# Reading one word per row group of four weight matrices at the start of a fused recurrence and FFN kernel

## The chip, the core and the metric

The kernel runs on one core of one Trainium2 chip. Five engines work side by side, each through its own list of instructions in order: TensorE (PE in the profile; PEld is its weight load), VectorE (DVE), ScalarE (ACT), GpSimd (POOL) and SyncE (SP), which here only issues DMAs. ScalarE also issues a few DMAs. All of them run on the same 16 DMA engines. The metric is the device time of one execution in microseconds, the median of several runs.

## The reference

Two stages follow one another. The first is a gated recurrence over 768 time steps for 4 batches and 8 heads of width 48; the second is a max-out feed-forward layer over the 3072 resulting tokens of width 384, with 768 hidden units.

```python
for t in range(S):
    state = alpha[:, :, t, :, None] * state + np.einsum('bhd,bhe->bhde', k[:, :, t], v[:, :, t])
    y[:, :, t] = np.einsum('bhd,bhde->bhe', q[:, :, t], state)
...
x = np.ascontiguousarray(attn_out.transpose(0, 2, 1, 3)).reshape(B * S, H * D)
h = np.maximum(np.maximum(x @ w1, x @ w2), x @ w3)
return (h @ w_out).astype(np.float32)
```

q, k, v and alpha are 4 x 8 x 768 x 48; w1, w2 and w3 are 384 x 768; w_out is 768 x 384. All are float32 in memory.

## The kernel before

The tokens are cut into 12 steps of 256 tokens. Step s is block s // 4 of time of batch s % 4, so the recurrence of a batch goes on four steps later. Inside a step the recurrence is worked in chunks: running sums of the logarithms of alpha (by a matmul with a triangle of ones), keys and queries scaled by the exponentials of these sums, scores and outputs by matmuls, and a state of 16-bit floats per batch that is updated by matmuls. The transposed output xT then goes through the three gate matmuls (`gate`, L396), a maximum on ScalarE and VectorE (`maxed`, L409 and L411) and the projection (`project`, L420), and is scaled and stored (`store`).

Each piece of work has a letter, and the order is written out by hand in three strings: `PROLOGUE` (L470, steps 0 to 2 with the early pieces of the following ones), `STEADY` and `LAST`. `@` gives the step. TensorE, VectorE, ScalarE, GpSimd and SyncE each run their own pieces in the order of these strings. `H` pieces are filler matmuls on a blank tile (`warm`, L440), a fixed number of them.

The pieces that stand at the start:

- `load` (L93) reads 256 tokens of one of alpha, q, k, v: 384 KB in pieces of 384 bytes, on SyncE's queue, into a ring of four buffers per tensor (ra, rq, rk, rv in the profile).
- `load_const` (L114) reads two constants on ScalarE's queue: `cp` (128 rows of 1032 bytes: triangle, identity and mask as 16-bit floats) and `c32` (128 rows of 16 bytes; c in the profile).
- the string at L118 sets the first order: alpha of step 0, the constants, then k, q and v of step 0. After that `PROLOGUE` issues alpha and k of step 1, alpha of step 2, q and v of step 1, alpha of step 3, k and q of step 2, alpha of step 4, and then the first four weight pieces (`K0 K2 K1 K6`).
- `load_weight` (L102) reads a weight piece of 384 KB on SyncE's queue into its own staging tile (ws); `cast_weight` (L160) turns it into 16-bit floats on ScalarE or GpSimd. The weights are read in twelve pieces; the first three of `w1`, `w2`, `w3` take columns 0 to 255 of every row.
- `pair_decay` (L184, tile pa) multiplies neighbouring alphas, `inverse` (L193, L195) and `logs` (L188, tile la) take logarithms and exponentials on ScalarE, `near_q` (L203) and `scaled` (L235, tile qk) form the scaled queries and keys, `values` (L156, tile vt) the scaled values, `sums` (L209) the sums on TensorE.

The tile layer gives each DMA one of eight semaphores in turn, over both queues together, in the order in which the DMAs are written. A DMA whose semaphore was used before waits, on its issuing engine, until the DMA eight places earlier has landed.

Of the kernel before, what the change touches and what calls it, by code (L numbers as in the profile page):

```python
# [9 lines left out]
FP32 = mybir.dt.float32  # L10
# [13 lines left out]
def kernel(  # L24
# [12 lines left out]
    nc = tc.nc  # L37
# [4 lines left out]
    P = 128  # L42
# [38 lines left out]
    cpool = ctx.enter_context(tc.tile_pool(name="const", bufs=1))  # L81
# [28 lines left out]

    cp = cpool.tile([P, 2 * P + 2 * U + R * P], FP16, name="cp")
    c32 = cpool.tile([P, 4], FP32, name="c32")

    def load_const(*_):  # L114
        nc.scalar.dma_start(cp, nc.inline_tensor(cp_np, name="cp").ap())
        nc.scalar.dma_start(c32, nc.inline_tensor(c32_np, name="c32").ap())

    for item in """  # L118
        a0 c k0 q0 v0
    """.split():  # L120
        if item[0] == "c":
            load_const()
        elif item[0] == "w":
            load_weight(int(item[1:]))
        else:
            load(item[0], int(item[1:]))
# [420 lines left out]
```

## Time and profile before

| | us |
|---|---|
| median of 11 runs | 156.33 |
| lowest and highest run | 154.99, 160.23 |
| profiled execution, its own time | 156.39 |
| its span, first to last instruction | 154.6 |
| TensorE busy | 145.7 |
| VectorE busy | 121.6 |
| GpSimd busy | 84.6 |
| ScalarE busy | 77.8 |

The DMA queues carry this (packets, MB, share of the time of 16 DMA engines; q1 is SyncE's queue, q10 ScalarE's, q8 the fetch of instructions):

```profile
q1 hardware_dynamic: 72576, 31.89, 82.9%
q8 instruction: 21, 0.34, 0.9%
q10 hardware_dynamic: 432, 0.23, 0.8%
```

In the profile a line of a timeline gives the start, the length, the engine, the line of the code, the operation and the tiles (out<-in); in brackets stands how long the engine was idle before, and what ended that. "SPq" and "ACTq" are the instruction queues of SyncE and ScalarE, where DMAs are issued: the length is that of the issue, not of the transfer. The 40 slices of the page are 3.9 us each.

### The profile page before, as it was taken

The numbers are of one execution on the slowest core, as the hardware profiler recorded it, in microseconds if no ns is written. First come the engines' busy times: TensorE is split into PE (matmuls) and PEld (weight loads), VectorE is DVE, ScalarE is ACT, GpSimd is POOL, SyncE is SP. The second block draws the span as 40 slices with busy tenths as digits, with TensorE's granted clock in tenths as the row PEclk, the third lists the DMA queues.
The fourth block names the chain that finished last, engine by engine and source line by source line (L and its number), as shares of the span: only waits on it lengthen the run. The fifth ranks groups of instructions, "written<-read, shape, count | busy, mean of one in ns | idle before, by whom it ended". The sixth has DMA issues, their size and how long they took to land.

```text
span 154.6 us, 6225 instructions
## 1 busy us (share of the span) xinstructions
PE 145.7 (94%) x2691; PEld 108.6 (70%) x2691; DVE 121.6 (79%) x212; ACT 77.8 (50%) x156; POOL 84.6 (55%) x123
## 2 busy tenths in 40 slices
PE   6999875999999999999999999999999999999990
PEld 2446453878877698687787786886877877868850
DVE  2256985899989789889799799697896995885560
ACT  3578945762773386383582573553835614132221
POOL 5328799736919307928848659379388573010000
PEclk9999999999999999999999999999999999999999
DMA  5999999999989899999999999999909609411023
GB/s 120 321 325 326 274 306 302 328 338 313 332 219 279 221 274 262 234 146 314 211 238 273 166 244 317 134 298 274 213 6 73 169 4 105 137 55 51 6 100 104
DMA packets 73035, 32.52 MB, mean 210 GB/s; under 512 B 65456, under 2 KB 73008, under 8 KB 73008
## 3 DMA queue, kind: packets, MB, share of 16 engines
q1 hardware_dynamic: 72576, 31.89, 82.9%
q8 instruction: 21, 0.34, 0.9%
q10 hardware_dynamic: 432, 0.23, 0.8%
q14 instruction: 6, 0.05, 0.1%
HBM read 23.73 MB, written 4.72 MB: 184 GB/s over the span
## 4 chain that ended last, share of the span: by engine, by line
PE 83%; DVE 4%; DMA 3%; SPq 2%; issue 2%; POOL 1%; ACT 1%; ACTq 0%; DVEq 0%; POOLq 0%
PE gps L396 47%; PE ops L420 15%; PE yps L330 6%; PE yps L311 4%; PE aps L280 4%; DMA ra<-in_alpha_dram 3%; PE sps L369 3%; PE tps L259 2%; SPq L95 2%; DVE lat L287 2%; PE wps L440 2%; POOL qk L235 1%; PE lps L209 1%; DVE pa L184 1%; ACT ob L156 1%
## 5 line engine op out<-in xcount | busy, mean ns | idle before, releaser
L396 PE MATMUL gps<-xT,wcat 128*128 128x256 f16 x648 | 78.0, 273 | 0.0
L396 PEld LDWEIGHTS <-wcat 128*128 128x128 f16 x648 | 60.8, 98 | 10.1 <-issue 0.3
L411 DVE TENSOR_TENSOR hT<-gps,h 128x512 f16<-128x512 f32 x36 | 24.4, 687 | 11.5 <-PE gps L396 11.4
L287 DVE TENSOR_TENSOR lat<-aps,cp 128x512 f16<-128x512 f32 x48 | 30.6, 679 | 2.0 <-PE aps L280 2.0
L156 ACT ACTIVATE ob<-ops,c 128x384 f32<-128x384 f32 (+1 forms) x21 | 12.1, 574 | 38.2 <-PE ops L420 37.3
L383 POOL TENSOR_TENSOR st<-full,gm 128x384 f16<-128x384 f32 x20 | 16.9, 847 | 18.1 <-DVE full L379 10.3
L411 DVE TENSOR_TENSOR h<-gps,h 128x512 f16<-128x512 f32 x36 | 24.0, 687 | 3.1 <-PE gps L396 1.0
L420 PE MATMUL ops<-wo,hT 128*128 128x384 f16 x144 | 26.5, 326 | 0.0
L420 PEld LDWEIGHTS <-hT 128*128 128x128 f16 x144 | 14.1, 98 | 7.3 <-DVE hT L411 0.2
L353 POOL TENSOR_TENSOR gt<-ge 128x4 f32<-128x4 f32 x17 | 4.2, 248 | 21.7 <-ACT ge L229 21.7
L150 ACT CAST xT<-yps 128x384 f16<-128x384 f32 x21 | 9.2, 481 | 12.1 <-PE yps L330 12.0
L440 PE MATMUL wps<-blank 128*128 128x512 f16 x47 | 13.6, 437 | 1.2 <-DVE blank L512 1.2
L150 ACT CAST h<-gps 128x512 f16<-128x512 f32 x16 | 9.3, 586 | 10.4 <-PE gps L396 7.2
L152 DVE CAST h<-gps 128x512 f16<-128x512 f32 x20 | 13.7, 685 | 1.0 <-PE gps L396 0.9
L330 PE MATMUL yps<-lat,vt 64*32 64x128 f16 x768 | 11.1, 220 | 1.7 <-issue 1.7
L235 POOL TENSOR_TENSOR qk<-ka,ic 128x384 f16<-128x384 f32 x11 | 11.2, 1019 | 0.5 <-ACT ic L217 0.4
L235 POOL TENSOR_TENSOR qk<-qa,ac 128x384 f16<-128x384 f32 x11 | 11.0, 999 | 0.2
L184 POOL TENSOR_TENSOR pa<-ra 128x384 f32<-128x384 f32 x9 | 9.0, 1002 | 3.5 <-DVE ka L199 3.5
L156 ACT ACTIVATE vt<-rv,c 128x768 f16<-128x768 f32 x11 | 10.3, 938 | 1.1 <-DMA rv<-in_v_dram 1.1
L330 PEld LDWEIGHTS <-vt 64*32 64x32 f16 x768 | 7.3, 90 | 4.2 <-issue 1.9
L235 POOL TENSOR_TENSOR qk<-rq,ac 128x384 f16<-128x384 f32 x10 | 10.0, 1002 | 0.0
L440 PEld LDWEIGHTS <-blank 128*128 128x128 f16 x47 | 4.7, 109 | 6.9 <-issue 3.0
(52 smaller groups left out, 168.5 us busy)
## 6 DMA issues: line engine op xcount, KB each, us to landing
ra<-in_alpha_dram SPq DMA_DIRECT2D x12, 384.0 KB, 5.0
rk<-in_k_dram SPq DMA_DIRECT2D x12, 384.0 KB, 5.1
rq<-in_q_dram SPq DMA_DIRECT2D x12, 384.0 KB, 5.5
rv<-in_v_dram SPq DMA_DIRECT2D x12, 384.0 KB, 5.3
out_dram<-ob SPq DMA_DIRECT2D x23, 192.0 KB, 3.9
ws<-in_moe_w_dram SPq DMA_DIRECT2D x9, 384.0 KB, 5.8
ws<-in_moe_w_out_dram SPq DMA_DIRECT2D x3, 384.0 KB, 6.3
qkT<-qk SPq DMA_TRANSPOSE x14, 4.4
```

The source lines that it names most:

```text
L150: nc.scalar.copy(out=dst, in_=src)
L152: engines[eng].tensor_copy(out=dst, in_=src)
L156: nc.scalar.mul(dst, src, col)
L184: engines[eng or "p"].tensor_mul(pair_of[s], raw("a", s, 0), raw("a", s, 1))
L235: engines[eng or "p"].tensor_mul(dst.rearrange("p a b c -> p (a b) c")[:, :, :D], near_of.pop((s, n)) if r == 0 else raw(n, s, 1), dec_of[ ...
L287: nc.vector.tensor_mul(lat_of[s, u][:, i].rearrange("p (a r) t -> p a r t", r=R), aps_of[s, u][i].rearrange("p (a r) t -> p a r t", r=R), ...
L330: nc.tensor.matmul(yps[x][C * m:C * (m + 1), f, :], vt[rows, r * HP + p].rearrange("p a b -> p (a b)")[:, at:at + C], lats[p // (HP // R)] ...
L383: engines[eng or "p"].tensor_mul(sts[s % B][1 - x].rearrange("p a (b d) -> p a b d", d=D), full_of.pop((s, x)), gm_of.pop((s, x)).unsqueez ...
L396: nc.tensor.matmul(gps[:, j, :], wcat[:, f, g, jj * P:(jj + 1) * P], xT[:, f].rearrange("p u t -> p (u t)"), start=(f == 0), stop=(f == NF ...
L411: nc.vector.tensor_max(h, gps, h_of[s, i - 1])
L420: nc.tensor.matmul(ops, hT_of[s][:, jj, u * P:(u + 1) * P], wo16[:, jj, :], start=(jj == 0), stop=(jj == NJ - 1))
L440: nc.tensor.matmul(wps, blank[:, :P], blank, start=True, stop=True)
```

## The change

A tile of 128 x 4 floats is added behind `c32`, and behind the constants four DMAs are issued on ScalarE's queue, one for each of `w1`, `w2`, `w3` and `w_out`. Each reads, for partition p, the first word of row 3p (row 6p for `w_out`): 128 words of 4 bytes, 9216 bytes apart. Nothing reads the tile. The weight loads themselves, their order and all other pieces stay as they are.

```diff
     cp = cpool.tile([P, 2 * P + 2 * U + R * P], FP16, name="cp")
     c32 = cpool.tile([P, 4], FP32, name="c32")
+    first_words = cpool.tile([P, 4], FP32, name="first_words")
 
     def load_const(*_):
         nc.scalar.dma_start(cp, nc.inline_tensor(cp_np, name="cp").ap())
         nc.scalar.dma_start(c32, nc.inline_tensor(c32_np, name="c32").ap())
+        for i, w in enumerate((moe_w1, moe_w2, moe_w3, moe_w_out)):
+            rows = w.shape[0] // P
+            nc.scalar.dma_start(first_words[:, i:i + 1], w.rearrange("(p n) m -> p n m", n=rows)[:, 0, :1])
```

In the built program the four DMAs take four places in the rotation of the eight semaphores. On SyncE's queue this changes which earlier DMA the first loads wait for:

```
load on SyncE's queue    waits before for     waits after for
q, step 0                -                    alpha, step 0
v, step 0                -                    cp
alpha, step 1            -                    c32
k, step 1                -                    first word of w1
alpha, step 2            alpha, step 0        k, step 0
q, step 1                cp                   first word of w2
v, step 1                c32                  first word of w3
alpha, step 3            k, step 0            first word of w_out
k, step 2, and later     the same DMA in both
```

The tiles allocated behind `c32` (la, qk, vt, the states and all work tiles) lie 32 bytes further on in SBUF.

## The prediction

> **What bounds the kernel now.** I read the slices and the chain of waits of the page first, then TensorE's waits over the first 50 us, then the start of ScalarE's and SyncE's timelines, then the records of single DMA packets in the trace.
>
> ```profile
> PE   6999875999999999999999999999999999999990
> DMA  5999999999989899999999999999909609411023
> ...
> PE 83%; DVE 4%; DMA 3%; SPq 2%; issue 2%; POOL 1%; ACT 1%; ACTq 0%; DVEq 0%; POOLq 0%
> ```
> TensorE is full from slice 8 to the end, at the full granted clock, and holds 83% of the chain. Only slices 1 to 7 (27 us) have gaps. The DMA engines are as full from slice 2 to slice 28. So a change at the start counts only through what it does to the moment from which TensorE never stops again, about 26.4 us.
>
> ```profile
> PE yps L330 <- issue: 1.7, 1, 1.7
> PE tps L259 <- POOL qk L235: 1.2, 3, 0.6
> PE wps L440 <- DVE blank L512: 1.2, 1, 1.2
> PE aps L280 <- DVE qkT L152: 0.3, 1, 0.3
> PE aps L280 <- DVE lat L287: 0.2, 1, 0.2
> PE lps L209 <- ACT la L188: 0.2, 1, 0.2
> ```
> These are all TensorE's waits from 0 to 50 us (total, times, longest). None is for a weight. One, 1.69 us from 24.75 to 26.44 us, is a wait for nothing in the program ("issue"); an instruction packet of 16 KB was in flight from 23.9 to 25.0 us, so I take it for a late refill of TensorE's instructions.
>
> ```profile
> 4.62 4.80 DMA ra<-in_alpha_dram
> 9.43 0.02 issue
> 9.45 0.57 DVE pa L184
> 10.02 0.02 issue
> 10.04 0.53 ACT la L188
> 10.57 0.04 issue
> 10.61 0.32 PE lps L209
> ```
> This is the chain early on (start, length, what). It runs through the second load of alpha (step 1), then VectorE's product at L184, which has L235's products for step 0 queued behind it, then ScalarE's logarithm, then TensorE. So what delays that load delays TensorE.
>
> ```profile
> 0.76 0.39 ACTq L115 DMA_DIRECT2D cp<-cp  x1
> 1.18 0.46 ACTq L116 DMA_DIRECT2D c<-c  x1
> 4.61 0.52 ACT L193 ACTIVATE ra<-ra 128x384 f32<-128x384 f32 x1 [2.59 <-DMA ra<-in_alpha_dram]
> ...
> 1.26 0.56 SPq L95 DMA_DIRECT2D rk<-in_k_dram  x1
> 1.87 1.47 SPq L95 DMA_DIRECT2D rq<-in_q_dram  x1
> 3.38 1.20 SPq L95 DMA_DIRECT2D rv<-in_v_dram  x1
> 4.62 1.15 SPq L95 DMA_DIRECT2D ra<-in_alpha_dram  x1
> ```
> ScalarE has issued its constants by 1.64 us and then waits until 4.61 us for alpha. SyncE issues a load in 0.46 to 0.56 us while the queue has room, and from the third on in 1.15 to 1.47 us, the pace of the transfers (384 KB in 1.2 us): it always has about two loads ahead.
>
> **The change part by part.** *Removed:* nothing. *Added:* four DMA issues on ScalarE's queue, four transfers of 128 packets of 4 bytes, a 16-byte tile. *Moved:* the tiles behind it in SBUF, by 32 bytes, and the rotation of DMA semaphores.
>
> *Issues.* The nearest row is c32, also 128 short pieces: 0.46 us. Four are 1.84 us, so ScalarE is free at 1.64 + 1.84 = 3.5 us. Its first work can't start before 4.61, so this costs nothing with 1.1 us to spare. Without that cover it would be 1.84 us; from below it is 0.
>
> *Packets.* By the packet records, c32's 128 packets of 16 bytes took 9 ns each, and so did its 16 semaphore packets: 144 x 9 / 16 engines = 0.081 us per transfer on every engine. The four make 0.32 us. From above I take the packets of cp (1032 bytes each, the first of the run, some over 500 ns): 101 ns on average, so 32 x 0.101 = 3.2 us on each engine. From below it is 0.25 us, at the 7 ns of the fastest semaphore packets. I take 9 ns, since these are short packets with an almost equal shape; what c32 does not have is addresses 9216 bytes apart.
>
> The Trainium skill ("DMA: Bandwidth & Descriptors", section Bandwidth) speaks against these reads: a transfer of 4 KB kept the DMA busy for 0.68 us in its table, and below 64 KB it calls transfers dominated by descriptors. By that the four would be an estimated 2.7 us one after the other, where c32's row gives 0.32. The row is of this chip's ScalarE queue beside a full stream, so it decides; but no row shows scattered words.
>
> *The semaphores.* The built program hands out eight DMA semaphores in turn over both queues, and each DMA waits for the one eight places before it. Before, the first SyncE load that waited was the seventh (alpha of step 2, for alpha of step 0, long landed). Now the third, q of step 0, waits for alpha of step 0. The later waits are for things that land earlier than their turn: v for cp, alpha 1 for c32, k of step 1 for the first word read. From k of step 2 on every DMA waits for the same one as before. Alpha 0's last semaphore count is at 4.59 us, so q's issue starts at about 4.65 and not at 1.87 us. What is late next: v, alpha 1 and all SyncE loads behind it. From an issue's start to its first packet I take cp's 1.0 us (0.77 to 1.77): q's packets start at 5.65 us. Before, they followed k's, which ended between 5.06 us on the first engine and 5.48 us on the last. The last engine sets the landing, so this alone is 5.65 - 5.48 = 0.17 us. With the stores' 0.82 us from issue to first packet it is 0 (5.47 us). If q's reads start as cold as cp's eight packets on an engine, (101 - 45 ns) x 8 = 0.45 us more. v is issued by 5.7 and alpha 1 by 6.3 us, each over a microsecond before its turn, so the stream is closed again.
>
> *Together.* The word packets are in ScalarE's queue by 3.5 + 0.6 = 4.1 us, so they run at the latest in the gap behind k, on the last engine from 5.48 to 5.80 us. The gap and the packets share time: q is late by the larger of 0.17 and 0.32 us. I take 0.33. The loads q, v, alpha 1 and all after them up to the weights ran gapless before (313 to 325 GB/s in each window of one or two microseconds from 3 to 16), so they keep this delay. ScalarE's, VectorE's and GpSimd's waits for q (7.13 us), v (8.32) and alpha 1 (9.45) each get longer by it, and TensorE's filler matmuls are a fixed number. The instruction refill is called for by TensorE's own progress and moves along.
>
> *The weights.* The words are read before them. Of their 1024-byte packets (median 46 ns) 50 took over three times that, 17.5 us in all; less 50 x 46 ns this is 15.2 us, or 0.95 us on 16 engines. That bounds what a prior touch can give the stream. But only ScalarE (2.7 us) and GpSimd (1.3 us) wait for weights: the first cast, at 22.04 to 22.87 us, is done before TensorE asks at 23.34 us. Also, the loads of q, k, v and alpha up to 15.9 us are first touches too and have no such packet, while the second group of weight loads (26.7 us), whose rows were touched by the first group, has 18. So I count 0, between -0.95 and 0.
>
> *The moved tiles.* The work tiles move by 32 bytes. One row shows such steps: gm's six buffers lie 32 bytes apart in the built program, and L355 on GpSimd takes 203 ns at the least and 204 in the median over all of them. So 1 ns is the size of it: 1 ns on each of L396's 648 matmuls would be 0.65 us above, and the same below. I take 0. DMA transposes and stores have slack: after slice 29 the DMA digits fall.
>
> *The sum.* The profiled execution took 156.39 us, its span is 154.6 and 1.8 lie around it; the median of the eleven runs is 156.33. 156.33 + 0.33 = 156.7 us.
>
> **The rivals.**
> *Slow words.* The scattered packets cost what cp's first packets cost. Place: ScalarE's turn between k and q of step 0. For: nothing in the trace reads addresses this far apart with so little in each packet, and cp shows what a first read can cost. Against: c32's 9 ns, and SyncE's first alpha load has no long packet. Price: up to 3.2 us, 159.6 us. It decides (over 0.78 us) from (0.78 - 0.04) / 32 = 23 ns per packet.
>
> *Weights found ready.* The touch takes away the 0.95 us of long packets, the DMA engines are less busy around 23.9 us, and the late instruction refill comes in time: 156.33 + 0.33 - 1.69 = 155.0 us. For: 20 long packets lie in the first weight load alone, and the refill packet took 1.12 us amid weight traffic. Against: TensorE waits for no weight, and loads to come fill the time gained.
>
> *Nothing arrives at TensorE.* The early waits take up 0.33 us, or the words are read without effect on anything: 156.3 us. For: the added waits are for things that mostly have landed. Against: the chain through alpha 1 shows no slack.
>
> **How the numbers follow.** Forecast 0.38, nothing arrives 0.08, slow words 0.34 (the cold start of q leads there too: 0.33 + 0.45 = 0.78), weights found ready 0.20. Under 0.5% (0.78 us) a measurement of this kernel can't be told from no change. So faster 0.20, same 0.46, slower 0.34. The forecast's own range is 156.3 to 157.1; to leave out no more than 2 in 10 it reaches down to 155.4, most of the way to 155.0, and up to 158.6, two thirds of the way to 159.6.
>
> **What would show it.** In the changed profile: four more issues of about 0.46 us on ScalarE's queue, ended by 3.6 us, and its first logarithm still at 4.6; 576 more packets on queue 10, with its share of 16 engines up by about 0.2 points; q's issue near 4.65 us; alpha 1 landing at about 9.75 and the product at L184 near 9.8 us; the first weight's cast about as late as before. I am wrong if alpha 1 lands over 0.8 us later, if ScalarE starts late, or if the 1.69 us wait is gone or has grown.

## The result, and the profile after

The changed kernel takes 158.64 us (median of 12 runs, 156.91 to 160.82) against 156.33 us before (47 runs): a ratio of 1.0153, with a 95% interval of 1.0117 to 1.0189. It is slower by about 2.3 us. Both profiled executions of it lie above its median (160.82 and 160.21 us), so stages are read from them and not the sum.

The page of the first, with the lines that answer to those of before:

```profile
span 159.0 us, 6229 instructions
...
PE   7969677799999999999998999899999999999990
...
DMA  5999999999999899999999999899811904811023
...
q10 hardware_dynamic: 1008, 0.23, 0.9%
...
PE 67%; DMA 9%; DVE 7%; POOL 7%; issue 3%; SPq 3%; ACT 1%; ACTq 0%; POOLq 0%
```

TensorE's gaps now end in slice 8, before in slice 7, and from there on it is nearly as full as before. The chain has moved: 9% of it are DMAs and 7% GpSimd where it was 3% and 1%. The 576 packets on queue 10 are there, at 0.1 points of the DMA time. The last of TensorE's early waits ends 3.1 us later than before. Here is that line from the timeline of the kernel before, and then from the changed one:

```profile
26.44 0.34 PE L330 MATMUL yps<-lat,vt 64*32 64x128 f16 x19 [1.69 <-issue]
```

```profile
29.58 0.34 PE L334 MATMUL yps<-lat,vt 64*32 64x128 f16 x19 [0.99 <-issue]
```

The span of this profile is 4.4 us longer than before (159.0 against 154.6). So in this profile most of the loss arises in the first 30 us; the rest arises later, and what causes it is not shown. ScalarE's and SyncE's timelines at the start (start, length, what):

```profile
0.76 0.39 ACTq L116 DMA_DIRECT2D cp<-cp  x1
1.18 0.46 ACTq L117 DMA_DIRECT2D c<-c  x1
1.67 1.45 ACTq L120 DMA_DIRECT2D first_words<-in_moe_w_dram  x3
3.14 0.45 ACTq L120 DMA_DIRECT2D first_words<-in_moe_w_out_dram  x1
4.41 0.53 ACT L197 ACTIVATE ra<-ra 128x384 f32<-128x384 f32 x1 [2.40 <-DMA ra<-in_alpha_dram]
```

```profile
1.25 0.57 SPq L95 DMA_DIRECT2D rk<-in_k_dram  x1
4.40 0.37 SPq L95 DMA_DIRECT2D rq<-in_q_dram  x1
4.82 0.58 SPq L95 DMA_DIRECT2D rv<-in_v_dram  x1
5.44 1.00 SPq L95 DMA_DIRECT2D ra<-in_alpha_dram  x1
```

ScalarE is not delayed: the four issues end at 3.6 us and its first logarithm starts at 4.41. SyncE has no line between 1.82 and 4.40 us. There, before, it issued q and v of step 0. Next come two of VectorE's products, one that waits for q and one that waits for alpha 1 (the alpha of step 1). Before, the second started at 9.45 us, and the first was this:

```profile
7.13 0.56 DVE L203 TENSOR_TENSOR qa<-rq,ra 128x384 f32<-128x384 f32 x1 [1.96 <-DMA rq<-in_q_dram]
```

In the changed kernel:

```profile
8.69 0.56 DVE L207 TENSOR_TENSOR qa<-rq,ra 128x384 f32<-128x384 f32 x1 [3.72 <-DMA rq<-in_q_dram]
11.02 0.56 DVE L188 TENSOR_TENSOR pa<-ra 128x384 f32<-128x384 f32 x1 [1.77 <-DMA ra<-in_alpha_dram]
```

Both are late by 1.6 us. TensorE's waits over the first 50 us now begin with that (total, times, longest); the wait of 1.6 us was 0.2 before:

```profile
PE lps L213 <- ACT la L192: 1.6, 1, 1.6
PE tps L263 <- POOL qk L239: 1.6, 2, 1.2
...
PE aps L284 <- DVE qkT L156: 1.1, 1, 1.1
PE yps L334 <- issue: 1.0, 1, 1.0
```

How the stream broke is best seen in windows of 0.5 us (busy time and number for each engine, then granted clock, DMA share, GB/s). Before, every one of the windows below has 323 to 326 GB/s, which is called the full rate in what follows. Two of them from before:

```profile
6.00:6.50 0.50, 0.50 (x6) 0.24 (x4) 0.00 (x0) 0.10 (x1) 0.50 (x1) 1.00 1.17 323
8.50:14.50 6.00, 5.77 (x79) 3.17 (x81) 4.14 (x8) 4.81 (x11) 2.47 (x5) 1.00 1.17 325
```

The changed kernel, first profile:

```profile
5.00:5.50 0.50, 0.50 (x3) 0.22 (x2) 0.00 (x0) 0.50 (x2) 0.00 (x0) 1.00 1.02 132
5.50:6.00 0.50, 0.50 (x3) 0.22 (x2) 0.00 (x0) 0.40 (x1) 0.07 (x1) 1.00 0.64 84
6.00:6.50 0.50, 0.50 (x3) 0.14 (x2) 0.00 (x0) 0.00 (x0) 0.50 (x1) 1.00 1.10 208
6.50:7.00 0.50, 0.50 (x7) 0.30 (x6) 0.00 (x0) 0.02 (x1) 0.43 (x1) 1.00 0.96 253
7.00:8.00 1.00, 1.00 (x6) 0.48 (x5) 0.00 (x0) 0.47 (x1) 0.39 (x1) 1.00 1.03 282
...
8.50:14.50 6.00, 4.45 (x65) 2.60 (x64) 3.80 (x8) 3.68 (x9) 0.35 (x2) 1.00 1.04 277
```

By the packet records k's packets end by 5.35 us and q's first comes at 5.45 us, near the forecast. But then the full rate is back only at 7.5 us, and from 9.5 us on the rate falls a second time. Finer windows of the same profile show both:

```profile
7.00:7.50 0.50, 0.50 (x4) 0.24 (x3) 0.00 (x0) 0.47 (x1) 0.00 (x0) 1.00 0.89 239
7.50:8.00 0.50, 0.50 (x4) 0.24 (x3) 0.00 (x0) 0.00 (x0) 0.39 (x1) 1.00 1.17 326
...
9.50:10.00 0.50, 0.50 (x4) 0.19 (x2) 0.00 (x0) 0.19 (x1) 0.00 (x0) 1.00 1.05 290
```

Against the windows of before, (191 + 242 + 115 + 72) x 0.5 + 43 = 353 KB are missing by 8 us, or 1.1 us of transfer. On the first engine alpha 1's last packet comes 1.0 us later than before, on the last engine 1.6 us later.

### The profile page after: what moved, and what is told of

Read it like the earlier page. It is cut to its first block, busy times and chain, and to the rows that moved or that the text cites. A ratio compares the mean times of both kernels' runs of the same rounds, so it can differ in the third digit from the quotient of the medians.

```text
span 159.0 us, 6229 instructions
## 1 busy us (share of the span) xinstructions
PE 146.6 (92%) x2691; PEld 108.9 (68%) x2691; DVE 124.2 (78%) x212; ACT 77.8 (49%) x156; POOL 84.4 (53%) x123
## 3 DMA queue, kind: packets, MB, share of 16 engines
HBM read 23.73 MB, written 4.72 MB: 179 GB/s over the span
## 4 chain that ended last, share of the span: by engine, by line
PE 67%; DMA 9%; DVE 7%; POOL 7%; issue 3%; SPq 3%; ACT 1%; ACTq 0%; POOLq 0%
PE gps L400 38%; PE ops L424 13%; DMA ra<-in_alpha_dram 6%; PE yps L334 5%; POOL qk L239 4%; PE yps L315 3%; DMA qkT<-qk 3%; PE aps L284 3%; DVE lat L291 3%; SPq L95 3%; PE sps L373 2%; PE tps L263 2%; POOL st L387 1%; DVE ka L203 1%; DVE gm L359 1%
## 5 line engine op out<-in xcount | busy, mean ns | idle before, releaser
L284 PE MATMUL aps<-qkT 48*64 48x128 f16 x384 | 9.0, 218 | 2.1 <-DVE qkT L156 1.1
```

What stands on the lines that cost most here:

```text
L284: nc.tensor.matmul(aps[i][cols, a * R + r, :], qkT[rows, r, 1, p, cols], qkT[rows, :, 0, p, cols], start=True, stop=True)
```

## The experiments

In the table the second column is the start of VectorE's product that waits for alpha 1, the third the rate of the DMA engines from 8.5 to 14.5 us, both from one profile. The first two rows are the kernel before and the changed one as in the section above. after_again is the changed kernel measured a second time, and each further row is an experiment described below. The ratios of all rows from after_again on are to runs of the kernel before on the same chip.

| kernel | alpha 1 product, us | GB/s | ratio to before (95%) |
|---|---|---|---|
| before | 9.45 | 325 | |
| changed | 11.02 | 277 | 1.0153 (1.0117 to 1.0189) |
| after_again | 10.51 | 324 | 1.0147 (1.0084 to 1.0209) |
| const4 | 10.59 | 275 | 1.0155 (1.0091 to 1.0218) |
| words2 | 9.48 | 325 | 1.0025 (0.9995 to 1.0056) |
| words3 | 9.76 | 325 | 0.9992 (0.9949 to 1.0035) |
| split | 9.90 | 319 | 1.0053 (1.0006 to 1.0100) |
| words4_plus1 | 9.88 | 325 | 1.0053 (1.0009 to 1.0097) |
| gap_alpha | 11.12 | 322 | 1.0091 (1.0049 to 1.0132) |
| gap_k | 11.16 | 324 | 1.0107 (1.0016 to 1.0198) |
| one_engine | 10.36 | 284 | 1.0119 (1.0069 to 1.0169) |
| alpha1_first | 8.31 | 325 | 0.9994 (0.9931 to 1.0057) |

### Is it the words, the wait, or the moved tiles?

**const4**, the changed kernel with constants read in place of the weights:

```diff
-        nc.scalar.dma_start(c32, nc.inline_tensor(c32_np, name="c32").ap())
-        for i, w in enumerate((moe_w1, moe_w2, moe_w3, moe_w_out)):
...
+        c32_dram = nc.inline_tensor(c32_np, name="c32").ap()
+        nc.scalar.dma_start(c32, c32_dram)
+        for i in range(4):
+            nc.scalar.dma_start(first_words[:, i:i + 1], c32_dram[:, i:i + 1])
```

> Four reads of the same shape (128 words of 4 bytes) in the same place, but from the constant c32 in place of the four weight matrices; no weight is touched early. Theory A (the added DMAs push the rotation of semaphores on, q of step 0 is issued only after alpha 0 has landed, SyncE's queue runs dry and its restart is slow): q issued at about 4.4 us, lands 1 to 2 us later than before, 1.5% slower than before like the changed kernel. Theory B (reading words scattered over the weights disturbs the reads that follow): within 0.5% of before, although q is issued late. Theory C (the 32 bytes by which the tiles move): slower by 1.5%, with q landing no later than about 7.4 us.

It loses as much, 1.0155. No word of a weight is read early, so the reading of scattered words is not what costs the time.

**words2** and **words3**, the changed kernel with fewer matrices:

```diff
-        for i, w in enumerate((moe_w1, moe_w2, moe_w3, moe_w_out)):
+        for i, w in enumerate((moe_w1, moe_w2)):  # words2
+        for i, w in enumerate((moe_w1, moe_w2, moe_w3)):  # words3
```

> Only w1 and w2 are touched, in the same place; the tile stays, so the tiles lie 32 bytes further as in the changed kernel. With two more DMAs no load of step 0 waits. Theory A: q issued at about 1.9 us, alpha 1 lands at 9.4 to 9.7 us, within 0.5% of before. Theory B: half of the loss, about 0.8% slower. Theory C: 1.5% slower.

> w1, w2 and w3 are touched, in the same place. Now v of step 0 waits for alpha 0, and q does not. Theory A: v is issued at about 4.4 us, when q still has over 1 us of transfer ahead, so the queue does not run dry: alpha 1 lands at 9.4 to 9.8 us and the time is within 0.6% of before. Theory B: three quarters of the loss, about 1.1% slower. Theory C: 1.5% slower.

Neither can be told from before, so the loss does not grow in step with the number of words; most of it appears with the fourth. Both have the tiles 32 bytes further on, which takes Theory C away. SyncE's timeline of words3 shows the same wait, one load later:

```profile
1.86 1.54 SPq L95 DMA_DIRECT2D rq<-in_q_dram  x1
4.63 0.37 SPq L95 DMA_DIRECT2D rv<-in_v_dram  x1
5.04 0.97 SPq L95 DMA_DIRECT2D ra<-in_alpha_dram  x1
```

v is issued 1.25 us later than before (3.38), and the time cannot be told from before (0.5% faster to 0.4% slower), because q's packets were still to come. What matters is not that a load is issued late but that the queue is empty then.

**words4_plus1**, the changed kernel with one more DMA behind the four (c32's address is named c32_dram for it, and the small tile is one column wider):

```diff
             nc.scalar.dma_start(first_words[:, i:i + 1], w.rearrange("(p n) m -> p n m", n=rows)[:, 0, :1])
+        nc.scalar.dma_start(first_words[:, 4:5], c32_dram[:, :1])
```

> All four words as in the changed kernel, in the same place, and one more read of 128 words of c32 behind them. The fifth added DMA takes the semaphore of alpha 0 and waits for it on ScalarE, which waits for alpha 0 anyway; q of step 0 then waits for cp (landed at 3.3 us) and not for alpha 0. Theory A (q's wait is the whole loss): q issued by 3.4 us, queue never dry, alpha 1 lands at 9.5 to 9.9 us; with ScalarE 0.45 us later at its first logarithm 0 to 0.6% slower than before, so about 1% faster than the changed kernel although it does more. Theory B (the words' reads, or more DMAs as such, cost the time): 1.5% to 2% slower than before.

It does more than the changed kernel and its measured time lies 1% nearer to that of before. SyncE's timeline shows why:

```profile
3.40 0.37 SPq L95 DMA_DIRECT2D rq<-in_q_dram  x1
4.78 0.37 SPq L95 DMA_DIRECT2D rv<-in_v_dram  x1
5.89 0.37 SPq L95 DMA_DIRECT2D ra<-in_alpha_dram  x1
```

q now waits for cp and goes out a microsecond earlier, while k is still under way. Two things can stand behind the 0.5% that is left, and no run separates them: the small packets, and ScalarE's first logarithm, which starts at 4.99 us in place of 4.61.

**split**, all four matrices touched before any weight is loaded, in two places where no load of step 0 waits for alpha 0 (`F` is a new piece that issues two of the reads, w1 and w2 behind the constants and w3 and w_out here):

```diff
-        H3@0 H1@0 H8@0 H1@0 m0v@0 r0@0 r1@0 l0@1 N0@0 l1@1 l0@2 c0@0
+        H3@0 H1@0 H8@0 H1@0 m0v@0 r0@0 r1@0 l0@1 N0@0 F2@0 l1@1 l0@2 c0@0
```

> All four matrices are touched ahead of all weight loads, w1 and w2 behind the constants, w3 and w_out on ScalarE's queue behind the first logarithms (about 6 us). No SyncE load of step 0 waits for alpha 0. Theory A: within 0.5% of before. Theory B: 1.5% slower. Theory C: 1.5% slower. If a prior touch helps the weight loads at all, it shows here: the first weight piece lands up to 0.6 us earlier and the time may be below that of before.

0.5% slower, with an interval from 0.1% to 1.0%, where all three theories had put it elsewhere or at the edge. So the four words, without the wait, cost something like the 0.5% of words4_plus1, or ScalarE's issues between its activations do. It shows no gain from the touch. From the issue of the first weight load to the first cast of a weight it takes 5.87 us (17.39 to 23.26), before 5.47 (16.57 to 22.04) and in const4, which touches no weight, 5.26 (18.07 to 23.33).

### A gap and nothing else

**gap_alpha** and **gap_k**, the kernel before with one small DMA on SyncE's queue that needs alpha 0 or k. The tile layer places DMAs by its own schedule; it puts the first ahead of q and the second ahead of v:

```diff
-        a0 c k0 q0 v0
+        a0 c k0 p q0 v0
...
+        elif item[0] == "p":
+            nc.sync.dma_start(stage[11][:, :1], rings["a"][0][:, 0, 0, :1])  # gap_k: rings["k"]
```

> No words, no further DMA on ScalarE's queue, tiles not moved. The kernel before with one DMA of 128 x 4 bytes from alpha 0's buffer on SyncE's queue between k and q of step 0: it needs alpha 0, so q is issued behind it at about 5.0 us and its packets start about 6.0 us, with some 0.6 us of empty queue on the last engine. If a dry queue alone is the cause: q lands 1.2 to 1.6 us late (0.6 us of gap and the slow restart), long packets before 15 us, 1.2% to 1.7% slower. If the four DMAs on ScalarE's queue are needed for it: q lands no more than 0.6 us late, below 0.6% slower.

> The same one load later: the small DMA reads k's buffer and stands between q and v of step 0, so v is issued at about 6.3 us and its packets start about 7.2 us, with some 0.6 us of empty queue behind q. Dry queue alone: q lands as before (7.0 us), v 1.0 to 1.6 us late, alpha 1 likewise, 1.0% to 1.7% slower. If only q's own delay matters: below 0.5%.

Both are about 1% slower, with no DMA added on ScalarE's queue and no tile moved. gap_alpha's 0.9% is below the 1.2% to 1.7% expected, though its interval reaches 1.3%. A dry queue alone therefore costs time, but these two runs do not show that it accounts for all of the changed kernel's 1.5%. gap_alpha's windows:

```profile
5.00:5.50 0.50, 0.50 (x3) 0.22 (x2) 0.00 (x0) 0.50 (x2) 0.00 (x0) 1.00 0.27 69
5.50:6.00 0.50, 0.50 (x3) 0.23 (x2) 0.00 (x0) 0.36 (x1) 0.29 (x1) 1.00 0.16 1
6.00:6.50 0.50, 0.50 (x3) 0.12 (x2) 0.00 (x0) 0.00 (x0) 0.50 (x1) 1.00 0.45 48
6.50:7.00 0.50, 0.50 (x8) 0.30 (x7) 0.00 (x0) 0.04 (x1) 0.20 (x1) 1.00 0.51 117
7.00:8.00 1.00, 1.00 (x6) 0.48 (x5) 0.00 (x0) 0.45 (x1) 0.41 (x1) 1.00 1.14 316
```

q was issued at 4.95 us. Its first packet comes at 6.20 us by the packet records, 1.25 us later, and until 7.0 us the engines move only 48 and 117 GB/s. At 7.0 us they are nearly back at the full rate. Missing are (254 + 325 + 275 + 208) x 0.5 + 9 = 540 KB, or 1.66 us at 325 GB/s; alpha 1's product starts 1.67 us later than before. The sum of the missing bytes is the delay.

### Why the stream can turn slow again

From 8.5 to 14.5 us the rate is 277 and 275 GB/s in the changed kernel's first profile and in const4; in after_again it is 324. In the first two the full rate had been back before (from 7.5 and 7.0 us), and the slow stretch begins at 9.5 us. So it is a second event and not the restart itself.

> The changed kernel once more, for a second profile beside the following three: 1.5% slower than before; q issued at about 4.4 us, alpha 1 landing at 10.4 to 11.1 us, and 384-byte packets of over 66 ns in the stream before 15 us, where before has none.

It came out so: alpha 1's product started at 10.51 us, and 15 packets took over 66 ns. But here the stream recovered by 7 us and kept the full rate. These are two of its windows:

```profile
6.00:6.50 0.50, 0.23 (x4) 0.16 (x4) 0.00 (x0) 0.22 (x1) 0.30 (x1) 1.00 0.63 122
6.50:7.00 0.50, 0.50 (x8) 0.26 (x7) 0.00 (x0) 0.29 (x1) 0.50 (x1) 1.00 1.13 311
```

So the low rate is not in every execution. A loss of about 1% does not seem to need it, since the profiles of gap_alpha and gap_k have 322 and 324 GB/s. Where it occurs, it costs TensorE more. Between TensorE's 100th and 200th matmul (14.4 and 19.3 us before) its delay against before grows from 1.57 to 3.18 us in the changed kernel's first profile and from 1.14 to 2.05 in const4. In after_again, gap_alpha and gap_k it changes by 0.1 us at most. How often the low rate occurs is not known, as each set of runs has one profile.

**one_engine**, the kernel before with extra work for a single DMA engine:

```diff
         nc.scalar.dma_start(c32, nc.inline_tensor(c32_np, name="c32").ap())
+        nc.scalar.dma_start(stage[11][:61, :96], moe_w_out[:61, :96])
```

> No words. The kernel before with one DMA behind c32 that puts 61 packets of 384 bytes on a single DMA engine, about 1.3 us of extra work there, with no gap in SyncE's queue and no wait moved onto alpha 0. It asks why the stream stays slow after the restart (277 GB/s from 8.5 to 14.5 us in the changed kernel against 325 before). Theory A1 (it is enough that the engines fall out of step): long packets before 15 us, 270 to 300 GB/s from 8.5 to 14.5 us, alpha 4 landing 2 us later or more, 1% to 1.6% slower. Theory A2 (only a dry queue brings the long packets): none before 15 us, 325 GB/s but for the one engine, alpha 1 and alpha 4 both about 1.3 us late, 0.6% to 1% slower.

Theory A1 fits: there is no gap in the queue, and still the rate falls from 7.5 us on (326 GB/s from 7.0 to 7.5 us, 242 from 7.5 to 8.0):

```profile
6.50:7.00 0.50, 0.50 (x4) 0.19 (x2) 0.00 (x0) 0.45 (x1) 0.50 (x1) 1.00 1.18 326
7.00:8.00 1.00, 1.00 (x6) 0.49 (x5) 0.00 (x0) 0.04 (x1) 0.92 (x2) 1.00 1.06 284
8.50:14.50 6.00, 4.67 (x67) 2.76 (x66) 3.93 (x8) 4.08 (x10) 0.81 (x1) 1.00 1.06 284
```

By the packet records 32 packets of 384 bytes took over 66 ns before 15 us, where before has none, the changed kernel 57 in its first profile. So the stream can lose rate without any gap. That the reason is engines out of step is an inference: what was changed is that one engine had more work. Between its 100th and 200th matmul TensorE's delay grows from 0.91 to 1.91 us here too.

### Does alpha 1 set the end?

**alpha1_first**, the kernel before with alpha 1 loaded ahead of v of step 0:

```diff
-        a0 c k0 q0 v0
+        a0 c k0 q0
...
-        H3@0 H1@0 H8@0 H1@0 m0v@0 r0@0 r1@0 l0@1 N0@0 l1@1 l0@2 c0@0
+        H3@0 H1@0 H8@0 H1@0 m0v@0 r0@0 r1@0 l0@1 l3@0 N0@0 l1@1 l0@2 c0@0
...
-        H1@0 k1v@0 V0@0 k0p@0 f0@0 l1@2 N0@1 l2@2 q0v@0 c0@1 H2@0 g0@0
+        H1@0 k1v@0 k0p@0 f0@0 l1@2 N0@1 l2@2 q0v@0 V0@0 c0@1 H2@0 g0@0
```

> No words. The kernel before with alpha of step 1 loaded ahead of v of step 0, and the scaled values of step 0 moved behind ScalarE's second logarithm accordingly. It tests the step that the landing of alpha 1 sets when TensorE gets going. If it does: alpha 1 lands at 8.2 us in place of 9.4, and the time falls by 0.5 to 1.2 us (0.3% to 0.8%). If the rest of the stream (q of step 2, alpha 4) sets it: within 0.3% of before.

The product starts at 8.31 in place of 9.45 us, as meant, and no change of the time is seen: 0.9994, from 0.7% faster to 0.6% slower, which leaves room for both forecasts. The trace shows where the lead goes. TensorE is 0.44 us ahead at its 100th matmul, but its next wait ends at 17.05 us, before at 17.00. Here are that wait and GpSimd's product of the next alpha (step 2) in alpha1_first:

```profile
17.05 0.62 PE L259 MATMUL tps<-cp,qk 128*128 128x128 f16 x8 [0.89 <-POOL qk L235]
12.05 1.00 POOL L184 TENSOR_TENSOR pa<-ra 128x384 f32<-128x384 f32 x1 [3.44 <-DMA ra<-in_alpha_dram]
```

Before:

```profile
17.00 0.62 PE L259 MATMUL tps<-cp,qk 128*128 128x128 f16 x8 [0.40 <-POOL qk L235]
```

The wait is for the scaled queries and keys (qk) that GpSimd makes, and GpSimd's work up to them begins with the alpha of step 2, which was not brought forward (12.05 us, before 12.00). So in this profile a later load sets the pace by 17 us. As the kernel also moves ScalarE's `V` piece, one profile does not prove it for every run.

## Why the prediction was wrong

*The issues* were right: 0.45 to 0.48 us each, over at 3.6 us, and ScalarE not delayed.

*The packets* were right: all 512 words took 9 ns. Where the queue does not run dry, they show as a delay of alpha 1's product: 0.31 us in words3 for an estimated 0.24 us of packets on each engine, 0.43 in words4_plus1 for 0.41, though only 0.03 in words2 for 0.16. The rival "slow words" therefore named the right side for a wrong reason; its place was ScalarE's turn, and const4 shows the same loss without scattered words.

*The semaphores* were right as a mechanism. q was issued at 4.40 and 4.72 us in the two profiles (forecast 4.65), and words3, words4_plus1 and the two gap kernels show that this wait at an empty queue is the larger part of the loss.

*Together* is the step that failed. It said that q is late by the larger of 0.17 us of gap and 0.32 us of packets. It took the time from q's issue to its first packet, 1.0 us, as the whole price of a restart, and put nothing into the sum for the time from the first packet to the full rate. The first part came as forecast: 1.05 and 1.04 us in the two profiles of the changed kernel. But from issue to full rate it is 1.8 us (after_again, 6.5 us) and 2.05 us (gap_alpha), and in the changed kernel's first profile 3.1 us (7.5 us). In place of 0.33 us the product that waits for alpha 1 came 1.06 and 1.57 us later.

The prediction had named a cold start of q (0.45 us) and left it out of the sum. Even with it, 0.78 us would have been too little, and it is not what was missing. Of q's first 512 packets those that took longer than the usual 22 ns add 0.35 and 0.11 us per engine in the two profiles. In gap_alpha's slow windows the DMA share is 0.45 and 0.51, against 1.17 before: for much of the restart engines carry no packet at all. A load has landed when its slowest engine has, and in the first profile q's last packets on the engines are spread over 1.2 us, in after_again over 0.5, before over 0.4.

*The stream is closed again* held in one profile of the changed kernel (324 GB/s from 8.5 to 14.5 us). In the other the rate fell again from 9.5 us on (277).

*The weights* counted 0, and nothing shows a gain: const4, without a touch, costs the same as the changed kernel. Of the 1024-byte packets 52 and 45 were long in the two profiles with the touch, 50 before, 19 in const4. So nothing is left for the rival "weights found ready".

*The moved tiles* counted 0, and words2 and words3 agree within their intervals.

*The instruction refill* was said to move along with TensorE. Reading the wait "issue" as a refill holds up: in the ten profiles that have this wait it ends 1.3 to 1.5 us after an instruction packet of 16 KB has come. But the packet does not keep its distance to TensorE's work. Against before it starts 1.13, 1.39 and 0.49 us later in gap_alpha, after_again and words2, while TensorE's 300th matmul, just ahead of the wait, is 1.68, 1.07 and 0.00 us late. So the wait gets shorter or longer. In gap_alpha it is 0.63 us shorter than before, and TensorE goes on only 1.06 us later than before:

```profile
27.50 0.34 PE L332 MATMUL yps<-lat,vt 64*32 64x128 f16 x19 [1.06 <-issue]
```

*The chain through alpha 1* was read too narrowly. A delay of alpha 1 with everything behind it costs time; alpha 1 alone, brought forward, gave no gain. Nor is the delay passed on one to one: gap_alpha's 1.67 us of delay cost 0.91%, about 1.4 us, while the changed kernel's 1.06 and 1.57 us stand beside 2.3 us. The difference to gap_alpha is some 0.6%. Two causes are possible: the 0.5% that words4_plus1 and split lose without the wait, and the low rate in some executions. The intervals are too wide to call either shown.

What stays open is why the engines start so slowly after a gap, why the stream sometimes turns slow again two microseconds later, and what exactly the words cost beside it. None of the kernels beats the one before beyond its interval.

## What to carry to other kernels

Before adding a DMA, however small, look in the built program at which earlier DMA each later one now waits for. Where semaphores are handed out in rotation, four tiny reads can make a large load on another queue wait for the first transfer of the kernel. A late issue cost nothing that could be measured here (words3) as long as the queue had work. A queue that ran dry cost, besides the wait for the first packet, another 0.7 to 0.8 us until the full rate was back (after_again, gap_alpha) and 2 us in the changed kernel's first profile. That should be a term of the sum of its own.

## What the runs showed of the hardware

- A load issued onto a dry queue had its first packet 1.04 to 1.25 us after its issue began. The full rate was back 1.8 us after it in after_again, 2.05 us in gap_alpha and 3.1 us in the changed kernel's first profile.
- Reading 512 words 9216 bytes apart took 9 ns a packet, as much as packets of 16 bytes from one block.
- Work of 61 packets for one DMA engine, about 1.3 us, lowered the stream of all engines from 325 to 284 GB/s between 8.5 and 14.5 us (one_engine, one profile).
- TensorE's wait for a late instruction refill ("issue") is not fixed: 1.69 us before, 0.99 and 1.97 in the two profiles of the changed kernel, 2.11 in words2. It ended 1.3 to 1.5 us after a 16 KB instruction packet had come. So two single profiles can differ by a microsecond at this point alone.
